# An explicit order for 3716 work units in an attention and MLP kernel on one core

## The chip, the cores and the metric

One core of one Trainium2 chip. The metric is the device time in microseconds (us) of one execution. The engines are TensorE (PE; its weight loads are PEld), VectorE (DVE), ScalarE (ACT), GpSimd (POOL) and SyncE (SP), which issues nearly all DMAs.

## What is computed

Linear attention with exponential features, whose output goes through an MLP with a SiLU. Cut to what matters:

```python
def phi(x):                                    # x: q or k, scaled; omega: 128 x 64
    proj = np.einsum('bhsd,md->bhsm', x, omega)
    h = proj - np.sum(x * x, axis=-1, keepdims=True) / 2.0
    h = h - np.max(h, axis=-1, keepdims=True)
    return np.exp(h) / np.sqrt(m)
kv = np.einsum('bhsm,bhsd->bhmd', k_p, v)
z = np.sum(k_p, axis=2)
num = np.einsum('bhsm,bhmd->bhsd', q_p, kv)
den = np.einsum('bhsm,bhm->bhs', q_p, z)[..., None] + 1e-06
x = num / den                                  # 4608 tokens x 512
h = x @ w_in                                   # 512 x 2048
g = h * (1.0 / (1.0 + np.exp(-h)))
out = g @ w_out                                # 2048 x 512
```

Batch 8, 8 heads, 576 positions, head size 64, 128 features, all in float32.

## The kernel before

The attention runs in 32 windows: window `n` holds one pair of heads of one batch entry. Per window TensorE projects k and q (`proj`, and `mid` or `mids` for the middle chunk), VectorE finds the row maxima and shifts (`top`, `nb`), ScalarE takes exponentials (`exp`, line 477; for windows 8 to 11 VectorE first subtracts in `low`, line 494, and ScalarE then runs `expall`), GpSimd sums k's features (`sums`, `esl`), TensorE spreads the sums (`z`), VectorE takes the denominators (`den`, line 560, with a reciprocal at line 566), GpSimd normalises (`norm`, line 571), TensorE transposes (`turn`, line 577), ScalarE copies (`en`, line 581), and TensorE multiplies keys with values of the next window and takes this window's numerators (`kvnum`, lines 536 and 598; `num` for the last one). ScalarE copies the result (`xh`, line 620), and for the first three token tiles VectorE keeps a remainder (`xl`, line 624).

The MLP works on nine token tiles of 512. Every float32 operand is split into a rounded part and a remainder, and a product takes three 128x512 matmuls (`thrice`, line 769). Tile 0 runs both stages directly (`s1`, `s2`), tiles 1 and 2 run `s1`, and pairs of tiles run through a seven-product scheme for 2x2 blocks (`deep` for the first layer, `pr` for the second). The operands of `deep` come from attention output by way of `xd` (a subtraction on VectorE, line 823), `ohi` (rounding on ScalarE, line 827) and `olo` (remainder on VectorE, line 831). In the first 200 us ScalarE, VectorE and GpSimd also rebuild and split the weights (lines 651 to 683), and in the first 500 us GpSimd forms sums of weight blocks (lines 702 to 741). Units `s1` and `s2` hold 3 matmuls of 128x512, units `pr` and `deep` 6; there are 3120 in all, in one fixed sequence for each stage.

No engine decides at run time: each takes its instructions in the order of its queue. That order is found when the program is built. The kernel adds 3716 units (933 on TensorE, 863 on ScalarE, 960 on VectorE, 423 on GpSimd, 537 on SyncE) to a `Plan`, each with its engine, a duration, the units it needs, the buffers it takes and frees, and a due time `key`. `Plan.run` then replays the program: per engine it looks at the units that can start, keeps those that could start within 0.25 us of the earliest one, and takes the one with the lowest key; over the engines it takes the unit that starts first. Before, the key is the due time, shifted for many units by pseudo-random amounts from a table `STIR` of some 200 entries, and raised by `STAY` where a unit needs another activation table than the last one:

```python
key = u["key"]
if u["table"] and u["table"] != table:
    key += STAY
...
p = min((p for p in pick if p[3] <= least + 0.25), key=lambda p: p[2:])
```

The replay knows that some VectorE units and all GpSimd elementwise units (`port=True`) exclude each other. PSUM has four banks `acc`, two `h` and two `att`; a unit with `banks` waits until the planner's replay has one free.

Of the kernel before, what the change touches and what calls it, by code (L numbers as in the profile page):

```python
# [77 lines left out]
STAY = 8.0  # L78
HANDOFF = {"PE": 0.3, "ACT": 0.25, "DVE": 0.22, "POOL": 0.2, "SP": 0.2}
CALM = 0.5  # L80
STIR = (
# [40 lines left out]
)  # L122
BOND = 0.0
TURN = 0.2
# [42 lines left out]
class Plan:  # L167
# [16 lines left out]
    def run(self):  # L184
        for n, u in self.units.items():
            key = u["key"]
            for seed, size, lo, hi, mask in STIR:
                if key < 900.0 and lo <= key < hi:
                    h = zlib.crc32((str(seed) + repr(n)).encode())
                    if not h & mask:  # L190
                        u["key"] += size * (h / 2**31 - 1)
# [53 lines left out]
        while any(ready.values()):  # L245
            best = None
            for e, us in ready.items():
                pick, least = None, None
                for u in us:
# [29 lines left out]
                    key = u["key"]  # L279
                    if u["table"] and u["table"] != table:  # L280
                        key += STAY
                    if e == "PE" and mode and tiled_by(u) == mode:
                        key -= BOND
# [49 lines left out]
        return order  # L333


@with_exitstack
def attention_mlp(ctx: ExitStack, tc: tile.TileContext, qS, kS, qT, kT, qn, kn, v, om_in, w_in, w_out, out):
# [581 lines left out]
    for n in range(NWIN):  # L919
# [3 lines left out]
        for i, who in enumerate("kq"):  # L923
# [9 lines left out]
            if fold:  # L933
                add(("r2",) + w, "ACT", 1.05, at(n, 2 * i - 4, 0), lambda n=n, who=who: square_raw(n, who), after=[("raw",) + w])
            else:
                before = [("nat", n, "k")] if i else ([("nat", n - 1, "q")] if n and n - 1 not in FOLD else [])
                add(("nat",) + w, "SP", 0.42, at(n, i - 13.5, 8.1 + 10 * i - 32), lambda n=n, who=who: load_nat(n, who),
                    order=before + [("raw",) + w], lat=0.95)
                add(("sq",) + w, "ACT", 0.59, at(n, 2 * i - 4, 13 + 10 * i - 32), lambda n=n, who=who: square(n, who),
                    after=[("nat",) + w])  # L940
                add(("ssum",) + w, "DVE", 0.67, at(n, 2 * i - 3, 14 + 10 * i - 32), lambda n=n, who=who: square_sum(n, who),
                    after=[("sq",) + w], order=[("ssum", n, "k")] if i else ([("ssum", n - 1, "q")] if n and n - 1 not in FOLD else []),
                    alloc=[] if i else [("sq", ("ss", n))])
# [26 lines left out]
        if not fold:  # L970
            add(("mids", n), "PE", 0.43, at(n, 2.9, 6.2 + 5.2), lambda ps, n=n: project_mids(n, ps), banks=1,
# [47 lines left out]
        add(zn, "PE", 0.3 if n < 12 else 0.25, at(n, 7, 32), lambda ps, n=n: zsum(n, ps), after=[("esl", n)] + e["q"], banks=1,  # L1019
# [23 lines left out]
        for g in range(3):  # L1043
# [3 lines left out]
            add(("turn", n, g), "PE", 0.6 if calm else 0.33, at(n, 9.5 + 0.1 * g, 44.2 + 0.8 * g), lambda ps, n=n, g=g: turn(n, g, ps),  # L1047
# [82 lines left out]
    def first(t, f):  # L1130
# [3 lines left out]
        for k in range(NK):  # L1134
            x = [("xl", NPAIR * t + k)]
            w = [("w1", t, f)] if t else [("wlo", "in", f)]
            add(("s1", t, f, k), "PE", 0.7 if t else 0.75, mm_time(pos), lambda k=k: stage1(t, f, k), after=x + w,
# [18 lines left out]
    def second(f):  # L1156
        nonlocal pos, prior
        for j in range(4):
            add(("s2", f, j), "PE", 0.7, mm_time(pos), lambda j=j: stage2(f, j), after=[("gl", f), ("wlo", "out", f)],
# [33 lines left out]
    def times(p, j, i):  # L1193
# [24 lines left out]
        add(me, "PE", 1.38, key, lambda: product(p, j, i), after=[("lo", p, j, u), ("w2", p, j, u)] + gate,  # L1218
# [99 lines left out]
    def level(p):  # L1318
# [4 lines left out]
        def part(s, j, i):  # L1323
# [9 lines left out]
            add(me, "PE", 1.38, mm_time(pos), lambda: deep(p, s, j, i), after=[("olo", p, j), w] + gate, order=[prior],  # L1333
# [138 lines left out]
```

## Time and profile before

| | |
|---|---|
| Median of 3 runs | 994.88 us (993.98 to 995.64) |
| The profiled execution: device time | 993.12 us |
| The profiled execution: span of instructions | 991.3 us |
| Mean granted TensorE clock | 0.989 |
| TensorE busy | 954.4 us (96%) |
| VectorE, ScalarE, GpSimd busy | 774.1, 651.4, 411.9 us |

The span runs from the first to the last instruction; the device time has 1.8 us more. TensorE is the engine that is busiest, but its matmuls are pipelined and their ends modelled, so the share says little by itself; a wait of TensorE is what an order can change. In the rows below a line of a timeline gives start, duration, engine, line, operation, tiles, count, and in brackets how long the engine had been idle and what ended that.

### The profile page before, as it was taken

What the parts mean: (1) busy time and instruction counts of PE and PEld (TensorE: products, weight loads), DVE (VectorE), ACT (ScalarE), POOL (GpSimd) and SP (SyncE); (2) the same over time, 40 slices, a digit from 0 to 9 for tenths busy, and PEclk for the clock granted to TensorE, in tenths of its full rate; (3) what the DMA queues carried; (4) which work ended last, traced back from release to release, by engine and by line L of the source; (5) the groups of instructions that cost most, each with busy time, mean ns of one, the idle gap of its engine ahead of it and who ended that gap; (6) DMA issues with size and microseconds to landing.
All of it is one profiled execution on the core that took longest, in us unless ns stands there. A gap on an engine that the chain in (4) does not pass through costs nothing.

```text
span 991.3 us, 16394 instructions
## 1 busy us (share of the span) xinstructions
PE 954.4 (96%) x5558; PEld 768.7 (78%) x5558; DVE 774.1 (78%) x1610; ACT 651.4 (66%) x1237; POOL 411.9 (42%) x430
## 2 busy tenths in 40 slices
PE   7898987999999999999999999999999999999998
PEld 6676766777778777887888878888888888888886
DVE  3898889669556698895888999878799966369954
ACT  8998865778797786768658966564374544325442
POOL 3675556577766655786622344332212210000000
PEclk9999999999999999999999999999999999999999
DMA  8479887799888887889676657675655566556562
GB/s 236 140 241 305 276 274 272 252 352 322 268 296 262 279 293 241 321 307 316 236 259 229 227 196 239 220 240 175 223 188 176 182 204 232 191 191 214 192 219 97
DMA packets 102707, 237.61 MB, mean 240 GB/s; under 512 B 13664, under 2 KB 44512, under 8 KB 102624
## 3 DMA queue, kind: packets, MB, share of 16 engines
q1 hardware_dynamic: 102480, 236.49, 71.4%
q8 instruction: 45, 0.74, 0.3%
q14 instruction: 38, 0.31, 0.1%
q10 hardware_dynamic: 144, 0.07, 0.0%
HBM read 192.48 MB, written 44.04 MB: 239 GB/s over the span
## 4 chain that ended last, share of the span: by engine, by line
PE 70%; DVE 13%; ACT 9%; DMA 4%; issue 2%; POOL 2%; SPq 0%; DVEq 0%; ACTq 0%; POOLq 0%
PE ps_acc L769 50%; PE ps_h L769 7%; PE ps_att L422 2%; DVE prod L560 2%; PE ps_att L536 2%; ACT hq L477 2%; DVE ts L815 2%; DMA w_d<-w 2%; PE ps_att L577 1%; ACT hk L477 1%; PE ps_h L422 1%; PE ps_att L598 1%; DVE g L663 1%; DVE g L665 1%; ACT in L410 1%
## 5 line engine op out<-in xcount | busy, mean ns | idle before, releaser
L769 PE MATMUL ps_acc<-ts,w 128*128 128x512 f32 x2544 | 614.8, 395 | 0.9 <-ACT en L581 0.4
L769 PEld LDWEIGHTS ps_acc<-ts,w 128*128 128x128 f32 x2544 | 469.5, 188 | 99.4 <-ACT en L581 0.9
L811 ACT CAST ts<-g 128x1024 fp32r<-128x1024 f32 x112 | 118.4, 1060 | 98.1 <-PE ps_acc L769 95.5
L815 DVE TENSOR_TENSOR ts<-g,ts 128x1024 fp32r<-128x1024 f32 x112 | 145.3, 1304 | 33.1 <-ACT ts L811 33.0
L769 PE MATMUL ps_h<-xq,w 128*128 128x512 f32 x576 | 151.2, 406 | 1.5 <-ACT g L802 1.5
L571 POOL TENSOR_TENSOR hq<-hq,rd 128x384 f32<-128x384 f32 x87 | 93.9, 1105 | 134.2 <-DVE rd L566 133.6
L769 PEld LDWEIGHTS ps_h<-xq,w 128*128 128x128 f32 x576 | 106.2, 192 | 24.1 <-ACT g L802 1.9
L861 DVE TENSOR_TENSOR g<-ps_acc,g 128x512 f32<-128x512 f32 x144 | 95.3, 684 | 27.0 <-PE ps_acc L769 25.4
L807 DVE TENSOR_TENSOR g<-g,g 128x1024 f32<-128x1024 f32 x64 | 83.9, 1329 | 11.2 <-ACT g L802 10.8
L506 POOL TENSOR_TENSOR t<-hk 128x256 f32<-128x256 f32 x64 | 55.0, 874 | 70.8 <-ACT hk L498 37.8
L560 DVE CUSTOM_DVE_ANT_0 prod<-hq,ps_att 128x128 f32<-128x128 f32 (+1 forms) x200 | 57.1, 286 | 9.5 <-PE ps_att L528 2.3
L519 POOL TENSOR_TENSOR es<-t,es 128x256 fp32r<-128x256 f32 x32 | 26.6, 832 | 86.0 <-ACT es L515 85.8
L683 POOL TENSOR_TENSOR w<-g,w 128x512 fp32r<-128x512 f32 x32 | 47.6, 1504 | 23.9 <-ACT w L679 17.7
L865 ACT ACTIVATE g<-g 128x1024 f32<-128x1024 f32 x36 | 37.6, 1057 | 26.9 <-DVE g L861 26.8
L406 DVE TENSOR_REDUCE sq<-in 128x9 f32<-128x576 f32 x48 | 35.2, 743 | 23.3 <-ACT in L401 23.0
L827 ACT CAST ts<-xq 128x1024 fp32r<-128x1024 f32 x21 | 22.2, 1058 | 44.2 <-PE ps_acc L769 43.0
L422 PE MATMUL ps_att<-oms,in 64*128 64x128 f32 x456 | 45.5, 281 | 0.0
L422 PEld LDWEIGHTS ps_att<-oms,in 64*128 64x128 f32 x456 | 39.9, 187 | 6.9 <-issue 4.6
L831 DVE TENSOR_TENSOR ts<-xq,ts 128x1024 fp32r<-128x1024 f32 x21 | 28.5, 1355 | 20.8 <-ACT ts L827 20.5
L511 POOL TENSOR_TENSOR t<-t,hk 64x128 f32<-64x128 f32 x64 | 37.6, 588 | 15.9 <-ACT hk L477 12.1
L401 ACT ACTIVATE in<-in 128x576 f32<-128x576 f32 x48 | 32.9, 697 | 12.7 <-DMA in<-kn 6.5
L888 DVE TENSOR_TENSOR c<-ps_acc,c 128x512 f32<-128x512 f32 x48 | 30.8, 680 | 6.7 <-PE ps_acc L769 6.1
(174 smaller groups left out, 1462.4 us busy)
## 6 DMA issues: line engine op xcount, KB each, us to landing
w<-w_d SPq DMA_DIRECT2D x168, 512.0 KB, 4.3
w<-ws_d SPq DMA_DIRECT2D x48, 512.0 KB, 4.2
v<-v SPq DMA_DIRECT2D x32, 320.0 KB, 4.5
out<-c SPq DMA_DIRECT2D x17, 512.0 KB, 4.2
in<-kT SPq DMA_DIRECT2D x24, 352.0 KB, 4.1
in<-qT SPq DMA_DIRECT2D x24, 352.0 KB, 5.4
g<-w_in SPq DMA_DIRECT2D x16, 512.0 KB, 4.6
g<-w_out SPq DMA_DIRECT2D x16, 512.0 KB, 5.3
```

The costliest lines, as they stand in the source:

```text
L422: nc.tensor.matmul(ps[:, cols], T["raw", n, who][r, o : o + P], oms[r], start=True, stop=True)
L506: nc.gpsimd.tensor_tensor(t[:, i], e[:, 5 * i : 5 * i + 2], e[:, 5 * i + 2 : 5 * i + 4], ALU.add)
L511: nc.gpsimd.tensor_tensor(t[r, i - 3, 0], t[r, i - 3, 0], e[r, MID], ALU.add)
L560: nc.vector.tensor_tensor_reduce(out=prod[r], in0=e[r, c], in1=z[r, j * M : (j + 1) * M], scale=1.0, scalar=GUARD, op0=ALU.mult, op1=ALU.a ...
L571: nc.gpsimd.tensor_tensor(e[:, c], e[:, c], rd[:, c].unsqueeze(2).broadcast_to([P, 3, M]), ALU.mult)
L683: nc.gpsimd.tensor_tensor(lo, T["w", i], hi.bitcast(F32), ALU.subtract)
L769: nc.tensor.matmul(ps, w(a), x[:, b], start=first and n == 0, stop=last and n == 2, **more)
L807: nc.vector.tensor_tensor(out, a, b, ALU.subtract)
L811: nc.scalar.copy(g[:, 0], T["g", p, SOURCE[j], u])
L815: nc.vector.tensor_tensor(g[:, 1], T["g", p, SOURCE[j], u], g[:, 0].bitcast(F32), ALU.subtract)
L861: nc.vector.tensor_tensor(to, T["q", p, chain, i], T["g", p, r, i // 2][:, i % 2], ALU.add)
L865: nc.scalar.activation(g, g, AF.Silu)
```

## The change

`STIR`, `STAY` and `BOND` go. A list `RANK` of 3716 numbers, a permutation of 0 to 3715, is laid beside the units in the order in which they are added, and the number takes the place of the due time as the key of the choice. Due times still decide from which PSUM pools a unit may take its banks. Some durations that the planner's replay uses are altered. The units, their instructions and their dependencies are the same.

```diff
-            for seed, size, lo, hi, mask in STIR:
-                if key < 900.0 and lo <= key < hi:
-                    h = zlib.crc32((str(seed) + repr(n)).encode())
-                    if not h & mask:
-                        u["key"] += size * (h / 2**31 - 1)
+        assert len(RANK) == len(self.units)
+        rank = dict(zip(self.units, RANK))
...
-                    key = u["key"]
-                    if u["table"] and u["table"] != table:
-                        key += STAY
-                    if e == "PE" and mode and tiled_by(u) == mode:
-                        key -= BOND
+                    key = rank[u["name"]]
...
+RANK = (
+    0, 1, 13, 2, 11, 15, 17, 19, 22, 23, 3, 14, 18, 25, 29, 30, 27, 24, 33, 31, 37, 42, 49, 6, 40, 41, 43, 47, 48, 51,
...
-TURN = 0.2
+TURN = 0.14
...
-                add(("r2",) + w, "ACT", 1.05, at(n, 2 * i - 4, 0), lambda n=n, who=who: square_raw(n, who), after=[("raw",) + w])
+                add(("r2",) + w, "ACT", 1.18, at(n, 2 * i - 4, 0), lambda n=n, who=who: square_raw(n, who), after=[("raw",) + w])
...
-            add(me, "PE", 1.38, mm_time(pos), lambda: deep(p, s, j, i), after=[("olo", p, j), w] + gate, order=[prior],
+            add(me, "PE", 1.365, mm_time(pos), lambda: deep(p, s, j, i), after=[("olo", p, j), w] + gate, order=[prior],
```

Where the list puts some of TensorE's attention steps, as the count of 128x512 products ahead of them, and where they stood before:

| Step | before | in the list |
|---|---|---|
| `kvnum(4)`, next step that takes banks | 72, `proj(6,k)` 84 | 96, `proj(6,q)` 120 |
| `proj(6,k)` | 84 | 45 |
| `proj(6,q)`, its `mid` | 132, 147 | 120, 141 |
| `proj(7,k)`, its `mid` | 198, 213 | 189, 225 |
| `proj(8,k)`, next attention step | 291, `turn(7,0)` 306 | 297, `z(7)` 333 |
| `kvnum(7)` | 354 | 387 |
| `kvnum(11)` | 573 | 582 |
| `kvnum(13)`, `kvnum(15)` | 729, 924 | 846, 1092 |
| `kvnum(17)`, first product that needs it | 1086, 1200 | 1200, 1200 |
| `z(19)`, `kvnum(19)`, first product that needs it | 1140, 1164, 1218 | 1218, 1218, 1218 |
| `kvnum(28)`, `num(31)` | 1956, 2412 | 1956, 2418 |
| Returns from attention steps to products | 176 | 169 |

## Rows read from the trace of the kernel before

**Rows 1.** Busy time by stretch: stretch, its length, PE, PEld, DVE, ACT, POOL, clock, DMA, GB/s.
```profile
70.60:482.00 411.40, 392.58 (x2409) 310.35 (x2409) 318.29 (x722) 315.02 (x627) 271.82 (x273) 0.98 0.86 290
482.00:991.30 509.30, 503.96 (x2723) 410.40 (x2721) 405.49 (x723) 271.10 (x443) 100.12 (x103) 1.00 0.61 205
```
**Rows 2.** TensorE's waits, whole span: who waited for whom, total us, times, longest.
```profile
PE ps_att L577 <- DVE hk L494: 4.9, 1, 4.9
PE ps_att L431 <- ACT hk L477: 4.3, 1, 4.3
...
PE ps_acc L528 <- ACT es L515: 3.0, 2, 2.8
...
PE ps_att L418 <- ACT xr L620: 2.3, 1, 2.3
PE ps_att L431 <- ACT hq L477: 2.1, 1, 2.1
```
**Rows 3.** Timeline, 166 to 174 us, around the longest wait.
```profile
166.76 3.15 POOL L683 TENSOR_TENSOR w<-g,w 128x512 fp32r<-128x512 f32 x2 [1.28 <-ACT w L679]
...
167.27 2.92 DVE L663 TENSOR_SCALAR g<-g 128x512 uint32<-128x512 uint32 x2
...
173.26 0.87 PE L577 MATMUL ps_att<-ident,hq 128*128 128x128 f32 x3 [4.90 <-DVE hk L494]
```
**Rows 4.** Two lines of the kernel: duration ns min/median/max, first and last start.
```profile
L571 POOL TENSOR_TENSOR hq<-hq,rd x87: 817/830/1902, 23.0 to 800.2; 128x384 f32<-128x384 f32 x87
...
L663 DVE TENSOR_SCALAR g<-g x32: 366/519/1545, 34.0 to 180.5; 128x512 uint32<-128x512 uint32 x32
```
**Rows 5.** Busy time in three stretches behind waits, columns as in rows 1.
```profile
92.70:96.10 3.40, 3.40 (x14) 3.01 (x13) 3.37 (x6) 2.82 (x5) 3.40 (x3) 0.50 1.02 371
...
140.40:143.90 3.50, 3.50 (x14) 2.91 (x14) 3.13 (x4) 2.60 (x8) 1.28 (x1) 0.51 0.76 175
...
173.20:178.10 4.90, 4.84 (x17) 4.29 (x18) 3.53 (x9) 2.56 (x5) 0.09 (x1) 0.51 0.26 80
```
**Rows 6.** Chain that ended last, 302 to 306 us: start, us, what.
```profile
302.70 1.59 PE ps_h L769 x6
304.29 1.36 PE ps_acc L769 x6
```
**Rows 7.** Timeline, 454 to 483 us: window 19 from `z` on, several engines.
```profile
454.62 0.40 PE L528 MATMUL ps_h<-es,ones 128*128 128x256 f32 x2
...
458.70 2.40 POOL L571 TENSOR_TENSOR hq<-hq,rd 128x384 f32<-128x384 f32 x3 [0.21 <-DVE rd L566]
...
462.70 0.49 PE L577 MATMUL ps_h<-ident,hq 128*128 128x128 f32 x3
...
463.28 0.54 ACT L581 COPY en<-ps_h 128x384 f32<-128x384 f32 x1
...
464.50 1.31 PE L536 MATMUL ps_h<-hk,v 128*64 128x128 f32 x20
...
466.71 3.02 PE L769 MATMUL ps_acc<-ts,w 128*128 128x512 f32 x12
...
467.46 0.60 ACT L620 COPY xq<-ps_att 128x512 f32<-128x512 f32 x1
...
468.09 2.39 DVE L823 TENSOR_TENSOR xq<-xq 128x1024 f32<-128x1024 f32 x2 [0.30 <-ACT xq L620]
...
471.56 1.05 ACT L827 CAST ts<-xq 128x1024 fp32r<-128x1024 f32 x1 [1.03 <-PE ps_acc L769]
...
474.12 1.34 DVE L831 TENSOR_TENSOR ts<-xq,ts 128x1024 fp32r<-128x1024 f32 x1 [0.17 <-issue]
...
475.47 0.37 PE L422 MATMUL ps_h<-oms,in 64*128 64x128 f32 x1
...
477.46 5.74 PE L769 MATMUL ps_acc<-ts,w 128*128 128x512 f32 x24
```
**Rows 8.** Group of instructions: count, busy us, mean ns of one, idle before.
```profile
L571 POOL TENSOR_TENSOR hq<-hq,rd 128x384 f32<-128x384 f32 x87 | 93.9, 1105 | 134.2 <-DVE rd L566 133.6 <-DVE nbm L455 0.6
```

More of the change, by code (lines that the diff above doesn't have):

```diff
@@ L1 @@
-import zlib
 from contextlib import ExitStack
@@ L77 @@
 SWITCH = 1.3
-STAY = 8.0
 HANDOFF = {"PE": 0.3, "ACT": 0.25, "DVE": 0.22, "POOL": 0.2, "SP": 0.2}
 CALM = 0.5
-STIR = (
[40 rows of a table removed]
-)
-BOND = 0.0
-TURN = 0.2
+TURN = 0.14
 LANDING = 0.9
@@ L184, in run @@
     def run(self):
-        for n, u in self.units.items():
-            key = u["key"]
-            for seed, size, lo, hi, mask in STIR:
-                if key < 900.0 and lo <= key < hi:
-                    h = zlib.crc32((str(seed) + repr(n)).encode())
-                    if not h & mask:
-                        u["key"] += size * (h / 2**31 - 1)
+        assert len(RANK) == len(self.units)
+        rank = dict(zip(self.units, RANK))
         end, first = {}, {}
@@ L278, in run @@
                                 t = b
-                    key = u["key"]
-                    if u["table"] and u["table"] != table:
-                        key += STAY
-                    if e == "PE" and mode and tiled_by(u) == mode:
-                        key -= BOND
+                    key = rank[u["name"]]
                     least = t if least is None else min(least, t)
@@ L333, in run @@
         return order
+RANK = (
[186 rows of a table added]
+)
 @with_exitstack
@@ L970, in attention_mlp @@
         if not fold:
-            add(("mids", n), "PE", 0.43, at(n, 2.9, 6.2 + 5.2), lambda ps, n=n: project_mids(n, ps), banks=1,
+            add(("mids", n), "PE", 0.37, at(n, 2.9, 6.2 + 5.2), lambda ps, n=n: project_mids(n, ps), banks=1,
                 after=[("raw", n, "k"), ("raw", n, "q"), "omega"], order=[("proj", n, "k")],
@@ L1018, in attention_mlp @@
         add(("esl", n), "POOL", 0.72, at(n, 6.4, 26.2), lambda n=n: sums_low(n), after=[("esh", n)], free=[("t", n)], port=True)
-        add(zn, "PE", 0.3 if n < 12 else 0.25, at(n, 7, 32), lambda ps, n=n: zsum(n, ps), after=[("esl", n)] + e["q"], banks=1,
+        add(zn, "PE", 0.24, at(n, 7, 32), lambda ps, n=n: zsum(n, ps), after=[("esl", n)] + e["q"], banks=1,
             order=[("z", n - 1)] if n else [], free=[("es", n)])
@@ L1046, in attention_mlp @@
                     after=[("den", n, 2)], order=[("norm", n, g - 1)] if g else [], free=[("rd", n)], port=True)
-            add(("turn", n, g), "PE", 0.6 if calm else 0.33, at(n, 9.5 + 0.1 * g, 44.2 + 0.8 * g), lambda ps, n=n, g=g: turn(n, g, ps),
+            add(("turn", n, g), "PE", 0.4 if calm else 0.28, at(n, 9.5 + 0.1 * g, 44.2 + 0.8 * g), lambda ps, n=n, g=g: turn(n, g, ps),
                 after=[("norm", n, 0 if one else g)], order=[("turn", n, g - 1)] if g else ([("turn", n - 1, 2)] if n else []),
@@ L1136, in first @@
             w = [("w1", t, f)] if t else [("wlo", "in", f)]
-            add(("s1", t, f, k), "PE", 0.7 if t else 0.75, mm_time(pos), lambda k=k: stage1(t, f, k), after=x + w,
+            add(("s1", t, f, k), "PE", 0.69 if t else 0.7, mm_time(pos), lambda k=k: stage1(t, f, k), after=x + w,
                 order=[done] if done else [], alloc=[] if k else [("h", ("ph", t, f))],
@@ L1158, in second @@
         for j in range(4):
-            add(("s2", f, j), "PE", 0.7, mm_time(pos), lambda j=j: stage2(f, j), after=[("gl", f), ("wlo", "out", f)],
+            add(("s2", f, j), "PE", 0.695, mm_time(pos), lambda j=j: stage2(f, j), after=[("gl", f), ("wlo", "out", f)],
                 order=[prior] if prior else [], alloc=[("acc", ("po", x)) for x in range(4)] if f == FIRST[0] and j == 0 else [],
@@ L1217, in times @@
         me = ("pr", p, j, i)
-        add(me, "PE", 1.38, key, lambda: product(p, j, i), after=[("lo", p, j, u), ("w2", p, j, u)] + gate,
+        add(me, "PE", 1.365, key, lambda: product(p, j, i), after=[("lo", p, j, u), ("w2", p, j, u)] + gate,
             order=[x for x in (prior, done) if x],
```

225 rows, old and new, of tables (RANK, STIR) are left out of this document.

## The prediction

> **What bounds the kernel now.** I first read the busy time of each engine before and after 482 us, then TensorE's waits in the earlier part, then the stretches around each long wait. After 482 us TensorE is busy in 503.96 of 509.3 us: nothing of weight is left there for an order to win. Between 70.6 and 482 us it is busy in 392.58 of 411.4 us and the granted clock is 0.98 instead of 1.00 [rows 1]. So the prize lies ahead of 482 us, in single waits: 4.9, 4.3, 2.3 and 2.1 us are the four longest behind 50 us [rows 2]. The reader is to see that each ends with a PSUM bank coming free, not with data: the two L431 waits end with the exponentials that read the banks of a projection, the 2.3 us one with a copy out of a bank, and the 4.9 us one with the subtraction `low` of window 8.
>
> The longest shows why such a bank is late. At 167.27 us VectorE runs two L663 in 2.92 us, beside two GpSimd L683 that run from 166.76 us for 3.15 us, and TensorE gets its bank at 173.26 us [rows 3]. L663 takes 0.37 us at its best, and GpSimd's L571 has a median of 0.83 us and a maximum of 1.90 us [rows 4]. VectorE's elementwise steps and GpSimd's hold each other up, and the order before queues the pair side by side. After three of the four waits the clock is at half speed for a while: 0.50, 0.51 and 0.51 with TensorE busy 3.40, 3.50 and 4.84 us [rows 5].
>
> **The change, part by part.** No instruction is added or removed; each of the 3716 units gets a number, and where several can start, the lowest goes first. I laid the numbers beside the units in the order in which the kernel adds them. No unit's number is below that of a unit it depends on, so the list reads as a complete schedule, and I take the queues to follow it. I count places in 128x512 products: `p300` has 300 of them ahead of it. On TensorE the same 194 attention steps (projections, transposes, key-value products) stand ahead of p1218 in both orders, so what counts is how long TensorE stands idle, or runs at half clock, on the way to p1218 and after it. One product takes 1.36/6 = 0.227 us [rows 6].
>
> *Waits taken away (S1).* The step that waited is moved away from the one whose bank it needs. The 4.3 us wait: `mid(7,k)` stands 15 products behind `proj(7,k)` before, 36 after, which is 21 x 0.227 = 4.8 us more, so it goes. The 4.9 us wait: the next attention step behind `proj(8,k)` comes after 15 products before and 36 after, 4.8 us more. The 2.3 us wait: `proj(6,k)` came 12 products behind the `kvnum(4)` whose bank it needed, and now stands ahead of it; the next step comes 24 behind, 2.7 us more. The 2.1 us wait: 15 products become 21, worth 1.4 us. Sum 4.3 + 4.8 + 2.3 + 1.4 = 12.8 us. What is late next is the same VectorE and GpSimd queue, at another place; that is U below.
>
> *Clock (S2).* Half speed costs half of the busy time: (3.40 + 3.50 + 4.84) / 2 = 5.9 us [rows 5], which goes if its three waits go.
>
> *Insertions (S3).* Six products behind a projection take 1.59 us, six others 1.36 us [rows 6], so coming back to the products costs 0.23 us. The list does so 169 times, before it was 176: 7 x 0.23 = 1.6 us.
>
> *New pile-up (C1, C2).* The windows from 13 on are put later, window 15 by 168 products and window 19's last step from p1164 to p1218, which is just where the product that needs it stands. The cover that window 19 had, 481.5 - 454.6 = 27 us from its `z` to that product, is gone, and the list leaves nothing else for TensorE. I price the chain from window 19 of the trace before [rows 7]. From `z` (454.62) past the denominators to the normalisation's start (458.70) 4.1 us; the normalisation itself 2.4; last transpose and its copy (462.70 to 463.82) 1.1; `kvnum` (464.50 to 466.71) 2.2; copies 0.6, and some 0.3 for the one ahead of it; rounding 1.05; its remainder 1.34; handoffs some 0.5. Sum 13.6 us. Beside it TensorE has `z` twice 0.5, two `kvnum` 4.4, three turns and two transposes some 1.2, and `proj(21)` (475.47 to 477.46) 2.0: 8.1 us. It waits 5.5 us. GpSimd's five sums of window 20 stand ahead of the normalisation and may add up to 1.6 us; I take half, so C2 = 6.3. At p1200 `kvnum(17)` stands directly ahead of the product that needs its result by way of copy, a subtraction (2.39/2 = 1.2 us), rounding and remainder: 2.2 + 0.9 + 1.3 + 1.15 + 1.6 = 7.2 us against 2.2 + 1.1 + 2.0 = 5.3 us of TensorE work, so C1 = 1.9.
>
> *Clock there (C3).* An idle time like those of 4 to 5 us before was followed by a half-speed stretch; one of 3.4 us costs 1.7 [rows 5].
>
> *Tight starts (C4).* `kvnum(11)` moves from p573 to p582, and the product at p585 needs its result: 2.2 + 0.7 + 0.7 (a remainder of half the size of L831's 1.34 us) + 0.25 = 3.85 us against 3.0 us of work, 0.9 us. At p387 the same chain meets 3.8 us of work: nothing.
>
> *Unseen (U).* The VectorE, ACT, GpSimd and SP queues are reordered everywhere, DMA issues included. What their new neighbours cost, the trace before doesn't show. The longest waits of the order before are 13.6 us for four [rows 2]; a fresh order may have between 0 and 9 us of that kind. The list spaces its TensorE steps as if it knew about the held-up pairs, so I take 4. The first 46 us are reordered too; the longest wait there that is not the start's own is 2.8 us [rows 2], so between -3 and +3 us, taken as 0. The tail behind p1956 moves by at most 48 products at its steps and keeps at least 30 products (6.8 us) between the last attention step and the level of products that needs it: 0.
>
> Sum: -12.8 - 5.9 - 1.6 + 6.3 + 1.9 + 1.7 + 0.9 + 4 = -5.5 us. Against the profiled execution (span 991.3, device time 993.12) that gives 987.6; the median of the runs is 1.76 us above it, so the forecast for the median is 989.4 us.
>
> **The rivals.**
> *Slower: the pile-up at p1200 to p1218.* It decides where the gain kept from S is below C + U. For it: the list places GpSimd's sums for windows 19 and 20, the weight sums and the normalisation within 18 products. If they and VectorE's remainders stretch as L571 does on the average (1105 ns [rows 8] to the median of 830 [rows 4], 1.33 times), C1 + C2 become 8.2 x 1.33 = 10.9, a second half-speed stretch adds 2.4, and C is 15.9. If in S the clock falls elsewhere in turn, S is 14.4. Then -14.4 + 15.9 + 4 = +5.5, 1000.4 us. Against it: in the order before, the same chain for window 19 met no stretched step. The Trainium skill (SBUF — State Buffer, section "SBUF: two separate sides") says that VectorE and GpSimd share one port pair as an exclusive lock, held for a whole instruction, and that the loser waits fully. By it the work on the pair can be moved but not lessened, which speaks against this change: windows put later bring their port work with them. The 2.92 us for two L663 [rows 3] agrees; that no gain can remain is not shown, since 4 to 5 us waits stood at single places.
> *No difference.* The new order has as many small waits as the old one: U = 9.5 in place of 4 gives 0, 994.9 us. For it: the order before came from a planner as well, and has its waits all the same.
> *The change doesn't do what it says.* The number decides only among units that the planner lets start within 0.25 us of the earliest one, by its own durations; the queues may leave the list. If so the pile-up may be spread: C falls to C3 and C4, 2.6, -20.3 + 2.6 + 4 = -13.7, 981.2 us.
>
> **How the numbers follow.** Forecast (989.4, from 983 to 992.8) 0.50; slower 0.28; no difference 0.15; list not followed 0.07, faster. About 0.2% (2 us) is what a measurement of this kernel can tell from no change. Faster 0.50 + 0.07 = 0.57, same 0.15, slower 0.28. The range takes the forecast's low side with C at 5 and U at 0 (some 980) and reaches over the slower rival, 1001.
>
> **What would show it.** Right: no wait over 1 us at L431 and L577 between 75 and 200 us; granted clock 1.00 there; in return a TensorE wait of 4 to 8 us ahead of a product at about 470 to 490 us with L831 as the releaser, and clock 0.5 behind it. p1218 should be reached some 5 us earlier than at 481.5, and from there to the end 509 to 510 us as before. Wrong: waits of 2 us and more at new places ahead of p1200 (U too small), or no wait at p1218 (list not followed).

## The result, and the profile after

The changed kernel takes 981.42 us (median of 4 runs, 978.92 to 981.68), the kernel before beside it 995.26 us (993.98 to 995.95). The ratio is 0.9857, with a 95% interval of 0.9837 to 0.9876. The forecast was 989.4 us: the direction was right, and the gain, 13.8 us, is more than twice the 5.5 us of the sum. The result lies below the forecast's own band (983 to 992.8), though within the whole range that was stated. The profiled execution of after has a span of 977.1 us, 14.2 us less than before.

In the profile of after every line number of the kernel is 136 higher than before: the products of L769 are now L905, L577 is L713, L571 is L707, L663 is L799, L669 is L805, L831 is L967. The queues that the program holds are the list itself, on all five engines.

Busy time by stretch of the kernel after, the answer to [rows 1] (stretch, its length, PE, PEld, DVE, ACT, POOL, clock, DMA, GB/s):

```profile
70.60:482.00 411.40, 401.36 (x2472) 319.92 (x2473) 322.45 (x742) 315.87 (x641) 272.63 (x276) 1.00 0.85 294
482.00:977.10 495.10, 490.84 (x2658) 399.37 (x2656) 396.82 (x710) 265.41 (x424) 90.18 (x96) 1.00 0.61 207
```

The earlier stretch holds 2472 matmuls in place of 2409, busy 401.36 us in place of 392.58, at a clock of 1.00 in place of 0.98. Behind it little has changed but its start. TensorE's waits of the kernel after over the whole span, the answer to [rows 2]:

```profile
PE ps_acc L713 <- POOL hq L707: 5.4, 3, 3.9
PE ps_att L554 <- ACT omn L513: 3.5, 1, 3.5
...
PE ps_h L664 <- ACT hq L613: 1.4, 1, 1.4
...
PE ps_acc L905 <- DVE ts L967: 0.9, 1, 0.9
PE ps_att L567 <- ACT hk L613: 0.7, 1, 0.7
```

The four waits of 2.1 to 4.9 us are gone, and GpSimd's L571, at 1105 ns on average in [rows 8], takes 1060 as L707; those of 3.5 and 3.9 us stand in the first 46 us, which both orders lose alike (17.3 and 17.5 us). The 1.4 us at L664 and the 0.9 us at L967 are new, and stand where the late windows pile up. TensorE there, in the kernel after (start, duration, engine, line, operation, tiles, count, idle time before and what ended it):

```profile
445.62 0.50 PE L905 MATMUL ps_acc<-ts,w 128*128 128x512 f32 x1 [0.38 <-ACT ts L963]
447.02 4.13 PE L905 MATMUL ps_acc<-ts,w 128*128 128x512 f32 x17 [0.90 <-DVE ts L967]
...
453.72 0.62 PE L664 MATMUL ps_h<-es,ones 128*128 128x256 f32 x2 [1.35 <-ACT hq L613]
454.75 2.40 PE L672 MATMUL ps_att<-hk,v 128*64 128x128 f32 x20 [0.41 <-ACT hk L613]
...
459.79 0.55 PE L713 MATMUL ps_h<-ident,hq 128*128 128x128 f32 x3 [0.69 <-POOL hq L707]
460.57 0.55 PE L713 MATMUL ps_att<-ident,hq 128*128 128x128 f32 x3 [0.24 <-POOL hq L707]
...
465.07 0.33 PE L680 MATMUL ps_att<-ident,kt 128*128 128x128 f32 x1 [0.42 <-ACT kt L677]
...
467.74 3.57 PE L905 MATMUL ps_acc<-ts,w 128*128 128x512 f32 x13
```

From `z(19)` at 453.72 us to the product p1218 at 467.74 us it is 14.0 us; the chain priced from [rows 7] had 13.6. The wait is not one of 4 to 8 us, as I had written, but eight of 0.2 to 1.4 us, and the clock falls behind the first of them:

```profile
453.90:457.40 3.50, 3.09 (x24) 2.56 (x25) 3.31 (x16) 3.02 (x11) 3.32 (x5) 0.51 0.90 258
```

Where the time went is read best by counting products. "Lost" is what lies between the starts of two TensorE instructions beyond the first one's usual pace (227 ns for a product, 103 to 119 ns for most attention matmuls), so it holds waits, returns to products and half speed alike:

| Products | lost before, us | lost after, us | difference | in the forecast |
|---|---|---|---|---|
| up to p24 | 23.8 | 23.9 | 0.1 | 0 |
| p25 to p240 | 16.7 | 4.2 | -12.5 | -11.5 |
| p241 to p576 | 19.1 | 9.2 | -9.9 | -6.3 |
| p577 to p1199 | 14.0 | 10.6 | -3.4 | 0 |
| p1200 to p1218 | 0.4 | 10.4 | +10.0 | +9.9 |
| the rest | 14.8 | 15.2 | +0.4 | 0 |
| returns (S3) and unseen (U), no place given | | | +2.4 |

The parts of the forecast are its own terms laid at their places: S1 with its half-speed stretches, C4 with the second stretch, and C1 to C3 (1.9 + 6.3 + 1.7 = 9.9) in the pile-up. The differences add up to -15.3 us, the span says -14.2: the pace is an average, so the two agree only roughly. With one pace for each kind of TensorE step, the same for both kernels (a quarter of its durations in the two traces are shorter), the six differences are +1.3, -12.7, -10.4, -3.5, +11.5 and +0.2. They add up to -13.8, the difference of the two traces from the first matmul to the last. So a row holds to some 1.5 us. In the first row the second count is the better one: p24 has the same steps ahead of it in both orders, and comes at 70.6 us before and at 71.9 after. What stands against the forecast is U.

### The profile page after: what moved, and what is told of

It reads as the page before. It is cut to its first block, busy times and chain, and to the rows that moved or that the text cites. A ratio compares the mean times of both kernels' runs of the same rounds, so it can differ in the third digit from the quotient of the medians.

```text
span 977.1 us, 16378 instructions
## 1 busy us (share of the span) xinstructions
PE 948.6 (97%) x5558; PEld 767.2 (79%) x5558; DVE 764.9 (78%) x1610; ACT 646.5 (66%) x1233; POOL 402.7 (41%) x430
## 4 chain that ended last, share of the span: by engine, by line
PE 80%; ACT 9%; DVE 8%; issue 1%; DMA 1%; POOL 0%; DVEq 0%; ACTq 0%; POOLq 0%
PE ps_acc L905 56%; PE ps_h L905 9%; PE ps_att L558 3%; PE ps_att L672 2%; ACT hk L613 2%; PE ps_att L713 2%; PE ps_h L558 1%; ACT hq L613 1%; ACT in L546 1%; PE ps_att L734 1%; DVE prod L696 1%; PE ps_h L734 1%; PE ps_h L713 1%; ACT g L787 1%; DVE g L997 1%
## 5 line engine op out<-in xcount | busy, mean ns | idle before, releaser
L905 PE MATMUL ps_acc<-ts,w 128*128 128x512 f32 x2544 | 612.1, 394 | 4.3 <-ACT ts L916 1.4
L905 PEld LDWEIGHTS ps_acc<-ts,w 128*128 128x128 f32 x2544 | 469.1, 188 | 104.2 <-ACT ts L916 1.9
L905 PE MATMUL ps_h<-xq,w 128*128 128x512 f32 x576 | 149.6, 400 | 0.1
L707 POOL TENSOR_TENSOR hq<-hq,rd 128x384 f32<-128x384 f32 x87 | 90.3, 1060 | 93.9 <-DVE rd L702 84.2
L905 PEld LDWEIGHTS ps_h<-xq,w 128*128 128x128 f32 x576 | 103.8, 188 | 21.6 <-DVE xq L760 0.4
L943 DVE TENSOR_TENSOR g<-g,g 128x1024 f32<-128x1024 f32 x64 | 88.1, 1390 | 5.1 <-ACT g L938 4.6
L819 POOL TENSOR_TENSOR w<-g,w 128x512 fp32r<-128x512 f32 x32 | 44.9, 1417 | 31.9 <-ACT w L815 15.7
L696 DVE CUSTOM_DVE_ANT_0 prod<-hq,ps_att 128x128 f32<-128x128 f32 (+1 forms) x150 | 42.9, 286 | 11.6 <-PE ps_att L664 6.8
L967 DVE TENSOR_TENSOR ts<-xq,ts 128x1024 fp32r<-128x1024 f32 x21 | 26.1, 1244 | 22.2 <-ACT ts L963 22.2
L696 DVE CUSTOM_DVE_ANT_0 prod<-hq,ps_h 128x128 f32<-128x128 f32 (+1 forms) x120 | 34.3, 286 | 6.1 <-PE ps_h L664 1.9
L862 POOL TENSOR_TENSOR ic<-ic 128x512 f32<-128x512 f32 x16 | 24.3, 1519 | 28.2 <-DMA ic<-w_d 15.9
L613 ACT ACTIVATE hk<-ps_att,nbk 128x128 f32<-128x128 f32 x117 | 33.9, 397 | 2.6 <-DVE nbk L592 2.2
```

The source lines that it names most:

```text
L613: nc.scalar.activation(h[:, c], ps[:, i * M : (i + 1) * M], AF.Exp, bias=bias_of(n, who, c), scale=-1.0 if n in FOLD else 1.0)
L696: nc.vector.tensor_tensor_reduce(out=prod[r], in0=e[r, c], in1=z[r, j * M : (j + 1) * M], scale=1.0, scalar=GUARD, op0=ALU.mult, op1=ALU.a ...
L707: nc.gpsimd.tensor_tensor(e[:, c], e[:, c], rd[:, c].unsqueeze(2).broadcast_to([P, 3, M]), ALU.mult)
L819: nc.gpsimd.tensor_tensor(lo, T["w", i], hi.bitcast(F32), ALU.subtract)
L905: nc.tensor.matmul(ps, w(a), x[:, b], start=first and n == 0, stop=last and n == 2, **more)
L943: nc.vector.tensor_tensor(out, a, b, ALU.subtract)
```

## The experiments

Seven of the twelve kernels take their order from a list that is followed strictly, so that any order can be given. Their edit is a new `RANK` and

```diff
-p = min((p for p in pick if p[3] <= least + 0.25), key=lambda p: p[2:])
-if best is None or p[3] < best[3]:
+p = min(pick, key=lambda p: p[2])
+if best is None or p[2] < best[2]:
```

**e1: the order of before, written as a list in the changed code.** 65 units get other PSUM banks that way, and two TensorE steps of window 13 stand six products later.

> The order before, engine by engine (PE: two steps around the 573rd product stand 6 products later, nothing else), given as a list in the changed code; the changed planner's durations choose the PSUM banks, and 65 units get others than before. Theory ORDER (the 13.8 us come from the order of the queues): 995 us, within 2 us of the kernel before. Rival BANKS (they come from the banks that the altered planner hands out): 988 us or less.

Measured: 999.19 us (10 runs), ratio 1.0023 (1.0008 to 1.0038). The altered planner constants, the banks and the list as such bring nothing, and rather cost some 2 us. The gain is in the order.

**e2 and e3: half of the change each.** e2 takes the changed order up to p576 and the order before from there; e3 the reverse.

> The changed order up to the 576th product, then what is left in the order before. By the traces the changed order gains 22.4 us of idle or half-speed time between the 25th and the 576th product, 3.4 us up to the 1200th, and gives back 10.0 at the 1200th to 1218th. Theory LOCAL (each part of the order has its own waits): the 576th product at 249 us as in the changed kernel, no pile-up at the 1218th, 5 to 8 us of new waits behind the seam, where the windows that were put later catch up: 979 to 982 us. Rival LOAD (the gain is work put off, which has to be paid behind the seam): waits of 12 us and more between the 576th and the 1200th product, 986 us or more.

> The order before up to the 576th product, then the changed order. Theory LOCAL: no early gain, the 576th product at 278 us; -3.4 + 10.0 us behind it, so 1001 us (998 to 1003), with 8 to 10 us of waits at the 1200th to 1218th product. Rival LOAD: with the windows ahead at the seam, the stretch behind it has less to do and the pile-up shrinks below 4 us: 990 to 995 us.

Measured: e2 982.01 us, ratio 0.986 (0.9841 to 0.988); e3 1002.83 us, ratio 1.0068 (1.0044 to 1.0091). The early part brings all of the gain and the late part costs. Yet e2 is no better than the whole change, although it leaves the pile-up out (0.4 us lost in p1200 to p1218, where e3 loses 9.9): it loses 14.0 us in p241 to p576 and 17.9 us in p577 to p1199, where the whole change loses 9.2 and 10.6. The windows that the changed order puts off have to be caught up somewhere. So e3 came out as LOCAL had it, and e2 has LOCAL's time without its reason: its 576th product comes at 261.6 us and not at 249, and behind it more is lost than in either of the two orders it is made of (14.0 and 10.6 us).

**e4: the four long waits alone.** The order and the banks of before, with seven TensorE steps put later, so that each of the four has the distance that S1 asks for, or more, from the step whose bank it needs: `proj(6,k)` from p84 to p96, `mid(6,k)` 99 to 114, `mid(6,q)` 147 to 156, `mid(7,k)` 213 to 240, the three `turn(7)` from 306, 309 and 315 to 327, 327 and 339. These are not the places that the change gives them (45, 63, 141, 225, and 372 for the three `turn(7)`). The other engines' steps keep their numbers, but those that now get their operands later are overtaken: 34 places of ScalarE's queue, 19 of VectorE's and 16 of SyncE's hold another step than before, GpSimd's none.

> The order before with seven TensorE steps put later and nothing else (banks as before): proj(6,k) 84 to 96, its mid 99 to 114, mid(6,q) 147 to 156, mid(7,k) 213 to 240, turn(7,0..2) 306, 309, 315 to 327, 327, 339 products; the steps of other engines that read them keep their place in the list. Theory SPACING: the waits of 2.3, 2.1, 4.3 and 4.9 us go with the half-speed stretches behind them, 18.7 us in all; some 5 us come back as waits of the next steps of the same windows: 981 us (977 to 985). Rival QUEUES (the banks are late because VectorE, ACT and GpSimd are late; whoever comes next waits): less than 6 us gained, 989 to 995 us.

Measured: 1001.58 us, ratio 1.0066 (1.0037 to 1.0096), slower than before. The profiled execution is the slowest of its five, 1007.44 us. TensorE's waits of e4 from 70 to 480 us (L621, L713, L762 and L954 answer to L436, L528, L577 and L769 of before):

```profile
PE ps_att L621 <- DVE hk L679: 3.6, 1, 3.6
PE ps_att L713 <- ACT hk L662: 2.8, 1, 2.8
PE ps_att L762 <- ACT hk L662: 2.6, 1, 2.6
PE ps_acc L954 <- DVE ts L970: 2.3, 1, 2.3
```

The waits stand elsewhere and are nearly as long: 18.7 us are lost in p25 to p240 and 25.3 in p241 to p576. I took that to show that the distance between two TensorE steps was the place where the loss showed and not its cause, and that another engine's time was missing. It doesn't show that much: the table below has e4's list late by its own plan, before anything is lost on the chip. It shows that these moves by themselves gain nothing.

Which engine's time might be missing, the planner's own clock helped to see. It is no measurement: it is the replay with planned durations by which the program was built. But laid beside the traces it tells where an order falls behind its plan (us at which a product starts, planned and in the trace):

| | p24 | p336 | p576 | p1223 |
|---|---|---|---|---|
| before | 67.9, 70.6 | 166.6, 185.1 | 258.2, 277.9 | 462.2, 482.8 |
| after | 70.2, 71.9 | 161.5, 165.0 | 243.4, 249.2 | 461.8, 469.3 |
| e4 | 67.9, 73.9 | 182.5, 195.0 | 274.9, 289.2 | 478.9, 497.3 |

By the plan both orders reach p1223 at the same time. On the chip the order before falls 15.8 us further behind between p24 and p336 (from 2.7 to 18.5), the changed one 1.8 us. So the attention that the changed order puts off brings 7.4 us from p24 to p336 (91.3 us planned against 98.7), and at p1223 the plans are level again. What lasts is how far the order before falls behind its plan: 14.0 us more than the changed one up to p336, 12.1 us more up to p1223. The altered durations don't make the difference: e1's list, which is the order before planned with them, has p1223 at 461.4 us and falls 16.0 us behind from p24 to p336. The list of e4 has p336 15.9 us later than before by its plan alone, and falls only 6.5 us behind, so e4 couldn't tell whether distance helps. In the trace of before VectorE lags ahead of TensorE (at 120 us of the plan by 9.4 us, TensorE by 7.2), and of some 25 us by which its steps planned for 64 to 160 us overran, the 70 weight steps (L663, L665, L669) account for 22.0; after, 77 of them account for 12.7 of some 16 us. The weight steps of the 32 blocks all stand ahead of p336 in the order before. In 70.6 to 190 us, of the kernel before:

```profile
70.60:190.00 119.40, 105.01 (x560) 83.78 (x560) 101.61 (x192) 88.59 (x172) 68.81 (x64) 0.94 0.80 271
```
```profile
L669 DVE SCALAR_TENSOR_TENSOR g<-g,g 128x512 uint32<-128x512 uint32 x25 | 25.0, 998 | 0.7
L663 DVE TENSOR_SCALAR g<-g 128x512 uint32<-128x512 uint32 x25 | 19.0, 775 | 0.0
```

and of the kernel after (second view: group of instructions, count, busy us, mean ns of one, idle before):

```profile
70.60:190.00 119.40, 115.91 (x652) 92.90 (x653) 99.27 (x222) 96.41 (x186) 72.84 (x70) 1.00 0.90 311
```
```profile
L805 DVE SCALAR_TENSOR_TENSOR g<-g,g 128x512 uint32<-128x512 uint32 x27 | 20.7, 783 | 0.4
L799 DVE TENSOR_SCALAR g<-g 128x512 uint32<-128x512 uint32 x25 | 14.3, 586 | 0.0
```

VectorE does 222 instructions in 99.27 us where it did 192 in 101.61: its weight steps are shorter. That gave a new theory, VECTORE, against QUEUES: TensorE's early waits are VectorE's time.

**e5 and e6: VectorE's third weight step left out, in both orders.**

```diff
-        else:
-            nc.vector.scalar_tensor_tensor(bits, high, 0x80000000, bits, ALU.bitwise_and, ALU.bitwise_or)
```

> The kernel before, its order unchanged, with the third of VectorE's three steps on each of the 32 weight blocks left out (the step that puts the sign bit in, so the weights lose their sign; it works in place on 128x512, and 25 of them took 25.0 us between 70.6 and 190 us of the trace of before, 998 ns each, against 783 ns in the trace of after). VECTORE: what the order of before loses between products 25 and 336 is VectorE's time, because its weight steps are stretched beside GpSimd's and the attention steps queue behind them. Taking 25 us off VectorE there takes most of the about 20 us away: 977 to 986, no wait of TensorE over 1.5 us between 75 and 200 us. QUEUES: the waits come from how the five queues are interleaved, whatever VectorE's steps last: at most 4 us faster, 991 to 996, and the four named waits are still there.

> The changed kernel with the same third step of VectorE on each weight block left out (the weights lose their sign). VECTORE: the changed order has only 4.2 us of lost time left between products 25 and 240 and 9.2 between 241 and 576, so it gains little: 975 to 981, and the gap to e5 is at most 7 us, where it was 14. QUEUES: the gap between the two orders stays 10 to 14 us.

Measured: e5 981.08 us, ratio 0.9838 (0.9815 to 0.9861); e6 979.60 us, ratio 0.9831 (0.9811 to 0.9852). The 14 us between the two orders have shrunk to 1.5. The same stretch, of e5 and then of e6:

```profile
70.60:190.00 119.40, 115.39 (x663) 91.69 (x662) 85.51 (x197) 95.65 (x188) 76.06 (x76) 1.00 0.91 314
```
```profile
70.60:190.00 119.40, 117.35 (x657) 94.68 (x657) 79.06 (x194) 95.85 (x188) 69.74 (x70) 0.99 0.90 312
```

With VectorE at 85.51 us the order before keeps TensorE as busy (115.39 us, clock 1.00) as the changed order does with VectorE at 99.27. The four waits have shrunk to 0.8 us and less, though no TensorE step was moved. Between p24 and p336 e5 falls no further behind its plan (2.3 us at p24, 2.2 at p336), though the plan still holds the step that was left out. QUEUES falls.

**e7: the changed order up to p240 only.**

> The changed order up to product 240, from there the order of before (a strict list). LOCAL, each stretch by itself: the 12.5 us of products 25 to 240 are gained, 3 to 6 us are given back where the order of before catches up behind product 240, and the rest is as in before: 985 to 990. WHOLE: the early gain is only lent, because attention steps are put off, and is given back when they are caught up: 993 to 997.

Measured: 998.50 us (10 runs), ratio 1.0012 (0.9995 to 1.0028): nearest to WHOLE, and a little above it. Up to p192 the trace is that of the changed kernel (126.9 us against 125.6); then the order before asks for what was put off, and TensorE waits. Its waits from 125 to 200 us:

```profile
PE ps_att L713 <- DVE hk L630: 4.9, 1, 4.9
PE ps_att L713 <- POOL hq L707: 4.5, 3, 3.9
PE ps_att L567 <- ACT hq L613: 1.6, 1, 1.6
```

p240 is reached at 149.3 us, against 151.0 before and 137.1 after. A large part of an early lead is lent: `kvnum(7)` starts at 191.9 us with 354 products ahead of it before, at 182.6 us with 387 after. The attention is 9.3 us earlier there, and TensorE has done 33 more products beside it (7.5 us of work). Those products are then missing at p1218, which I take to be the pile-up; no run separates that.

**e8: the opposite dose.** The changed kernel with the third weight step issued twice.

```diff
+            for _ in range(2):
                 nc.vector.scalar_tensor_tensor(bits, high, 0x80000000, bits, ALU.bitwise_and, ALU.bitwise_or)
```

> The changed kernel with the third of VectorE's steps on each weight block issued twice (the second time it writes the same bits again): some 20 us more for VectorE between 75 and 200 us (27 steps of 0.69 to 0.9 us), nothing else. VECTORE: the changed order keeps TensorE busy only as long as VectorE keeps up; VectorE is busy 99.3 of 119.4 us there, so 20 us fill it, and the waits that the change took away come back: 987 to 997. QUEUES: VectorE's load is of no account there: at most 4 us slower, 980 to 985.

Measured: 1006.42 us, ratio 1.0074 (1.0045 to 1.0102), dearer than either theory had it. That is 25 us above the changed kernel's median, and some 22 us by the two ratios (the kernel before was 3.3 us slower beside e8 than beside the changed kernel). Its VectorE in the same stretch:

```profile
70.60:190.00 119.40, 101.95 (x510) 80.46 (x509) 111.58 (x210) 85.05 (x165) 61.32 (x54) 0.94 0.76 255
```
```profile
L806 DVE SCALAR_TENSOR_TENSOR g<-g,g 128x512 uint32<-128x512 uint32 x52 | 45.3, 881 | 1.3
```

The step takes 45.3 us in place of 20.7, 24.6 us more, and p24 to p576 takes 201.2 us in place of 177.3, 23.9 us more. Added time of VectorE goes through nearly one to one. So the changed order has no reserve: it stands just at the point where VectorE keeps up, and e6 shows that there is hardly anything to be had beyond it.

**e11 and e12: GpSimd's share.** That GpSimd's running beside is what lengthens VectorE's weight steps was so far an inference. Of the 25 L663 behind 64 us of the trace of before, the 9 with no GpSimd instruction beside them have a median of 417 ns, the other 16 one of 912; for L669 it is 691 (13) and 1202 (13). So GpSimd's own weight step was cut to a quarter, in both orders:

```diff
         nc.scalar.copy(parts_of(i)[0], T["w", i])
+        nc.scalar.copy(parts_of(i)[1][:, P:], T["w", i][:, P:])
...
-        nc.gpsimd.tensor_tensor(lo, T["w", i], hi.bitcast(F32), ALU.subtract)
+        nc.gpsimd.tensor_tensor(lo[:, :P], T["w", i][:, :P], hi.bitcast(F32)[:, :P], ALU.subtract)
```

> The kernel before, its order unchanged; GpSimd's step that makes the low part of each weight block (128x512, 27 of them for 40.4 us between 70.6 and 190 us of the trace of before) does 128x128 only, and ScalarE fills the other columns with a copy of the weights (so three quarters of the low parts are wrong). GpSimd has some 28 us less there, ScalarE some 12 us more, VectorE's steps are the same. BESIDE: VectorE's weight steps are long because GpSimd's run beside them; their means in that stretch fall from 775 ns to under 600 for the first step and from 998 to under 830 for the third, and the time to 980 to 989. ALONE: their length has another cause; the means stay within 5%, and the time is 992 to 1004 (ScalarE's 12 us).

> The changed kernel with the same two edits (three quarters of the low parts are wrong). BESIDE: the changed order has little left to gain in that stretch, 976 to 984, and the gap to e11 is at most 7 us. ALONE: the gap between the orders stays 10 to 16 us.

Measured: e11 990.01 us, ratio 0.9949 (0.9931 to 0.9967); e12 986.03 us, ratio 0.99 (0.9885 to 0.9915). VectorE's steps and the stretch, of e11:

```profile
L669 DVE SCALAR_TENSOR_TENSOR g<-g,g 128x512 uint32<-128x512 uint32 x25 | 19.2, 766 | 0.7
L663 DVE TENSOR_SCALAR g<-g 128x512 uint32<-128x512 uint32 x25 | 13.4, 553 | 0.0
```
```profile
70.60:190.00 119.40, 109.34 (x617) 85.49 (x616) 91.18 (x203) 105.84 (x213) 49.34 (x69) 1.00 0.87 294
```

Nothing of VectorE's was changed, and its means fell from 998 to 766 and from 775 to 553 ns: BESIDE. Between p24 and p336 e11 falls 6.9 us behind its plan, where the order before falls 15.8. The gap between the orders falls to 4.0 us. Both times lie just above what I had expected, since ScalarE, with the copies put on it, is now the fullest engine beside TensorE (105.84 of 119.4 us). The time is therefore no clean price of the stretching; the durations are.

**e9 and e10: a list that beats both?** From e2's list (and, for e10, from one that turns to the order before at p720), single steps were moved wherever the planner's clock ended earlier.

> A new strict list: that of e2 (changed order to product 576, then the order before), with single steps and steps of one window moved by up to some tens of places wherever that made the planner's own clock end earlier; the clock was run with the planned durations and again with VectorE's and GpSimd's 4% longer. On that clock product 1223 starts 12 us earlier than with e2's list. CARRIES: the clock fell behind the chip by only 2 us between products 24 and 336 of the changed kernel, so most of the 12 us are seen: 968 to 975, product 1223 at 458 to 464 us. TOO TIGHT: a list fitted to the clock leaves no room, and what it gains there comes back as waits: 978 to 985.

> As e9, found from the list that follows the changed order to product 720 and then the order before; on the planner's clock product 1223 starts 10 us earlier than with e2's list. CARRIES: 969 to 976. TOO TIGHT: 978 to 985. The lists of e9 and e10 differ in hundreds of places, so a gain of both is not one list's luck.

Measured: e9 979.10 us, ratio 0.9804 (0.9778 to 0.9829); e10 984.93 us, ratio 0.9868 (0.9837 to 0.9899): TOO TIGHT. On its clock e9 starts p1223 at 449.6 us, 10.0 us ahead of e2's 459.6 (I had written 12); on the chip at 470.4 us against 471.4. It falls behind all the way, 4.1 us at p24, 9.6 at p336, 20.8 at p1223, with all engines lagging alike. e9's ratio is the lowest measured, but it was not run beside the changed kernel, and 979.1 against 981.4 us is about what can just be told apart. I don't claim that it is better.

## Why the forecast was right in direction and wrong in size

**What held.** The four waits and the half-speed stretches behind them (S1, S2) are gone, and the granted clock is 1.00 in 75 to 200 us. The pile-up (C1, C2, C3) came at 10.0 us (11.5 with one pace) for 9.9, with 2.40 us for the normalisation and 1.22 for L967 where [rows 7] had 2.40 and 1.34. From p1218 to the end of the span it is 977.1 - 467.7 = 509.4 us, within the 509 to 510 written down.

**The step that failed: U.** "What their new neighbours cost, the trace before doesn't show", I wrote, and took +4 us of new waits, from 0 to 9. In its place the small losses went down too. Without U the sum is -9.5 us; the profiled execution has -14.2. So U was in effect -4.7 us, outside its own bounds, 8.7 us from the value taken. I had bounded it from one side only: a rearranged queue can hold fewer neighbours of the bad kind, and the rows for that were before me. [rows 3] shows two L663 at 2.92 us and [rows 4] shows 0.37 at best; between them lies time that an order may give back. VectorE was busy 101.61 of 119.4 us in 70.6 to 190 us, and that stretch's own row would have pointed to it behind the banks; I read only the whole of 70.6 to 482 us, where it is 318.29 of 411.4 [rows 1]. The share alone doesn't decide it, since after, with 99.27 us, TensorE hardly waits; e5 and e8 do.

**A step that came out right for a wrong reason: S1.** I gave each wait its own cure, so many products put between two TensorE steps. e4 gives such distances and is slower, though its list was late by its own plan. e5 makes no such move and is rid of the waits. The 12.8 us were there to be had, but taking time off VectorE is enough to get them.

**A term that was too large: S3.** The 0.23 us of a return to the products came from one place. Over the 63 places in the trace of before where six products of one unit follow an attention step and more products follow them, the six take 1.475 us in the median against 1.36, so 0.12 us each, and seven of them 0.8 us in place of 1.6.

**p1218.** I had it some 5 us earlier than 481.5; it came at 467.74, 13.8 us earlier. All of the gain is won ahead of it.

**The rivals.** *Slower* did not come: C stayed near 10 because the steps that I had priced were not stretched (the normalisation of window 19 takes 2.40 us for three, as in [rows 7]). It leaned on the Trainium skill (SBUF — State Buffer, section "SBUF: two separate sides"), whose exclusive lock I took to mean that work on the pair can be moved but not lessened. That was my reading, not its rule. The trace of before agrees with the rule where L663 is longest, 1545 ns: it starts 0.04 us behind an L683 of 1296 ns and ends 0.29 us behind it.

```profile
80.68 1.30 POOL L683 TENSOR_TENSOR w<-g,w 128x512 fp32r<-128x512 f32 x1 [4.46 <-ACT w L679]
80.71 1.54 DVE L663 TENSOR_SCALAR g<-g 128x512 uint32<-128x512 uint32 x1
```

What one engine waits depends on which steps meet, and the order decides that: L669's mean of 998 ns became 783 with no instruction changed. *No difference* is out by the interval. *List not followed* had priced 981.2 us, beside the result, but its reason is wrong: the queues are the list's, and the pile-up is there.

**What stays open.** By the plans the later attention is paid back by p1223, and the changed order's gain is the 12 to 14 us that it falls less behind; 9.3 us of these (22.0 against 12.7) are VectorE's weight steps, and the rest has no shown cause. That split leans on the planner's replay: e11 has the shorter steps in the order before, but a fuller ScalarE beside them. The 31 to 37 us (by the pace that is taken) that after, e2 and e9 all lose between p25 and p1218, each at other places, have no shown cause either.

## What to carry to other kernels

A wait of the busiest engine names the step that ended last, not the engine that is short of time: look at the busy share of every engine in the stretch of the waits alone, and above all compare the durations there of one and the same instruction with its shortest. Moving the waiting steps by themselves brought other waits here, and a list changed by hand has first to be looked at by its own plan; taking away time of the suspected engine in both versions, and adding it in the better one, tells in three runs whether that engine is the bound. An order that runs ahead by putting work off has to be followed to the place where that work is due, and a plan without slack in it gives on the chip what the plan before gave.

## What the runs showed of the hardware

GpSimd and VectorE lengthen each other far more than I had reckoned with: L663 takes 417 ns alone (median) and up to 1545 ns beside GpSimd. It goes the other way too: GpSimd's L683 takes from 1272 to 1749 ns in the trace of before, and with a quarter of the columns, in e11, from 453 to 916, where the only one with no VectorE instruction beside it took 457. Of before, and then of e11, in 70.6 to 190 us:

```profile
L683 POOL TENSOR_TENSOR w<-g,w 128x512 fp32r<-128x512 f32 x27 | 40.4, 1516 | 23.9 <-ACT w L679 17.7 <-PE ps_acc L769 5.9
L684 POOL TENSOR_TENSOR w<-g,w 128x128 fp32r<-128x128 f32 x28 | 17.8, 646 | 29.0 <-ACT w L679 27.5 <-DMA w_d<-w 1.3
```

TensorE's granted clock was 0.94 on average in 70.6 to 190 us before, with the three half-speed stretches of [rows 5] behind waits, and 1.00 in the same stretch of e5, where no wait is longer than 0.8 us.
